# A deep-and-cross network on one core: the row products of the long run split into four products on 32x32 tiles

## The chip, the core and the metric

The kernel runs on one core of one Trainium2 chip. The metric is device time in microseconds (us) for one launch, the median of several runs; lower is better. A profile of one execution lies beside it: a page of tables, and a trace that can be asked for single stretches of time, lines and engines.

## What is computed

Six cross layers over a batch of 16384 rows of 416 features in bfloat16. The reference, cut to what matters:

```python
# x0: (16384, 416), ws: (6, 416, 416), bs: (6, 416), all bf16
x = x0
for l in range(6):
    proj = jnp.einsum('bd,de->be', x, ws[l]) + bs[l]
    x = x0 * proj + x
return x
```

Per layer this is one matrix product with 416 x 416 weights, a bias, a multiplication with x0 and an addition. 416 is 3 x 128 + 32: three full tiles of features and a tail of 32.

## The kernel before, in words

**Layout.** The batch is cut into eight groups of 2048 rows (`GC`), each group into four chunks of 512 rows (`CH`, index j). Activations are kept transposed, features on partitions and batch rows along the free axis, so a product of one layer takes a piece of the weights as the loaded operand and a chunk of 512 rows as the moving operand, and leaves 512 f32 in one PSUM bank. The three full feature tiles lie in `xs` (index t); the tails of the four chunks of a group are stacked as four blocks of 32 partitions in `x3s`. The weights lie in `wm` (three full tiles of input features) and in `w3` (the 32 tail features, four copies, one in each block of 32 partitions).

**Jobs and tiles.** A job is one layer l of one group g. It makes three output tiles of 128 features (i = 0, 1, 2), each in four chunks, and one tail of 32 features. Jobs of different groups are interleaved in a fixed diagonal order. An output chunk needs 416 input features. In the long middle part of the program it is made from row products only: the array is used as four strips of 32 rows and 128 columns, and a product takes 32 input features of one strip r (partitions 32r to 32r+31) against 128 output features. Three full tiles give three such products in each of the four strips, and the tail gives one more in the strip where it lies: 13 products into one bank.

**The searched run.** The function `stream` (line 1005) writes this part. The order of its products is the string `ORDER` (line 204), a result of a search: each letter names a strip and a chunk begun some places ago, and stands for that strip's three or four products of that chunk. `replay` (line 230) turns the string into a list of products by time, with 20 ticks for a product (`SLOT`) and 22 ticks (`FENCE`) between the end of one strip's products of a chunk and the start of the next strip's, as both add into the same bank. In the program the same rule is a semaphore: `Program.add` (line 35) leaves out a dependency between two TensorE instructions on one bank when they have the same `row`, and keeps it as a wait when their rows differ. The run holds 6504 row products: 6000 from line 1040 (full tiles) and 504 from line 1044 (tail features). When a chunk's last product is queued, `evacuate_chunk` (line 538) queues ScalarE's copy from PSUM with the bias (line 550) and, for pairs of chunks, VectorE's multiplication (line 562) and addition (line 567).

**Tail phases.** A "|" in `ORDER` is a tail phase: `tails` (line 677) makes the 32 tail features of two or three jobs. It has 12 products per job on strips of 32 columns and all 128 rows (line 697, form 128*32), and then its corners, four products per job of 32 input by 32 output features (line 685, form 32*32). After the corners the run goes on. There are 14 such phases in the run.

**Elsewhere.** Ahead of the run and behind it the work is done with full products (line 650), row products by `rows32` (line 671, or split in four on 32x32 tiles in its `small` form, line 665) and column products (line 638). The last job is done with batch rows on partitions (line 1130 and after).

**Engines and queues.** TensorE's instructions are in program order; every product is a weight load and a matmul, two instructions. ScalarE and VectorE empty PSUM, SyncE issues nearly all transfers. All waits are semaphores that `Program._solve` places.

The lines that the change touches, with the functions around them:

Of the kernel before, what the change touches and what calls it, by code (L numbers as in the profile page):

```python
# [4 lines left out]
CH = 512  # L5
T32 = 32
# [15 lines left out]
class Program:  # L22
# [12 lines left out]
    def add(self, eng, fn, reads=(), writes=(), lane=None, batch=None, hold=False, release=False, row=None):  # L35
        op = Op(eng, fn, lane, batch, row)
        deps = {}
        if eng == "pool":
            writes = list(writes) + ["pool"]
        for t in reads:  # L40
            w = self.writer.get(t)
            if w is not None:
                deps[id(w)] = (w, True)
        for t in writes:
            w = self.writer.get(t)
            if w is not None:
                deps[id(w)] = (w, True)
            for r in self.readers.get(t, ()):
                if id(r) not in deps:
                    deps[id(r)] = (r, False)  # L50
        for d, raw in deps.values():
            if d.lane is None and d.eng == eng and lane is None and (eng == "pe" or not raw):
                if row is None or d.row is None or row == d.row:
                    continue
            op.deps.append(d)
        for t in reads:
            self.readers.setdefault(t, []).append(op)
        for t in writes:
            self.writer[t] = op
            self.readers[t] = []  # L60
        if eng == "dve":
            if hold:
                self.flush()
                self.held = op
            else:
                self.queue[eng].append(op)
                if release:
                    self.flush()
        else:
            self.queue[eng].append(op)  # L70
        if lane is not None:
            batches = self.lanes.setdefault(lane, [])
            if not batches or batches[-1][0] != batch:
                batches.append((batch, []))
            batches[-1][1].append(op)
        return op
# [229 lines left out]
def bass_standalone__cross_network_dcn__recsys_kernel(  # L306
# [33 lines left out]
    wm = [nc.alloc_sbuf_tensor(f"wm_{l}", [P, NT, D], BF16) for l in range(L)]  # L340
    w3 = [nc.alloc_sbuf_tensor(f"w3_{l}", [P, D], BF16) for l in range(L)]
# [13 lines left out]
    psum = nc.alloc_psum_tensor("ps", [P, 8 * CH], FP32)  # L355

    pr = Program(nc)
    add = pr.add
# [16 lines left out]
    def bank(b, p0=0, p1=P, n=CH):  # L375
        return psum[p0:p1, b * CH:b * CH + n]
# [18 lines left out]
    def wm_tok(l, i):  # L395
        return ("wm", l) if i < 2 else ("wm", l, "rest")
# [41 lines left out]
    def quad(g, l, j):  # L438
        q = (j + turn_of(g, l)) % NJ
        return q, slice(q * T32, (q + 1) * T32)  # L440
# [14 lines left out]
    def x_src(g, l):  # L455

        if l == 0:
            s = slot(g)
            return lambda t, a, b: x0s[s][:, t * GC + a * CH:t * GC + b * CH], lambda t, j: x0_tok(s, t, j)
        s = xset[(g, l)]  # L460
        return lambda t, a, b: xs[s][:, t * GC + a * CH:t * GC + b * CH], lambda t, j: ("x", s, t, j)

    def x3_src(g, l):
        if l == 0:
            s = slot(g)
            return x0s[s][:, XW:XW + CH], x03_toks(s)
        s = xtail[(g, l)]
        return x3s[s][:, :], [("x3", s)]
# [264 lines left out]
    def load_nat(j, k0, k1):  # L733
# [6 lines left out]
        reads=["warm"], writes=["warm"])  # L740
# [229 lines left out]
    def start_job(g, l, ahead=True):  # L970
        started.add((g, l))
        if ahead:
            xset[(g, l + 1)] = free_x.pop(0)
        if (g, l) in W_LOAD:
            load_wm(W_LOAD[(g, l)], "sp")
            load_w3(W_LOAD[(g, l)], "sp")
        if (g, l) in G_LOAD:
            load_group(G_LOAD[(g, l)])
# [26 lines left out]
    def stream(run, keep, part):  # L1005

        chunks = [(it[1], it[2], j) for it in run if it[0] == "tile" for j in range(NJ)]
        due, n = [], 0
        for it in run:
            if it[0] == "tails":  # L1010
                due.append((n, it[1]))
            else:
                n += NJ
        tiles = [it[1:] for it in run if it[0] == "tile"]
        place = {it: NJ * k for k, it in enumerate(tiles)}
        needs = [[(t, place[(g, l - 1), t]) for t in range(NT if c < len(chunks) - keep else part)
                  if c - place.get(((g, l - 1), t), -99) < 30] for c, ((g, l), i, j) in enumerate(chunks)]
        plan, read, left = replay([quad(g, l, j)[0] for (g, l), i, j in chunks], [len(b) for n, b in due],
                                  needs, keep, part)
        at = list(ring)  # L1020
        plan = [(t, r, c, at[b]) if r >= 0 else (t, r, [at[k] for k in c], b) for t, r, c, b in plan]
        left = [at[k] for k in left]
        phases.extend(on for _, r, _, on in plan if r < 0)
        count, seen = {}, {}
        for _, r, c, b in plan:
            if r < 0:
                dve[0] = max(dve[0], phases.pop(0)) + PAIR * len(behind_tail) + TAILS
                tails(due.pop(0)[1], corners_last=True, banks=c)
                continue
            (g, l), i, j = chunks[c]  # L1030
            if (g, l) not in started:
                start_job(g, l, ahead=False)
            count[c] = count.get(c, 0) + 1
            q, ecols = slice(r * T32, (r + 1) * T32), slice(i * P, (i + 1) * P)
            t = seen[c, r] = seen.get((c, r), -1) + 1
            src, stok = x_src(g, l)
            s3, tok3 = x3_src(g, l)
            kw = dict(start=count[c] == 1, stop=count[c] == 4 * NT + 1, tile_position=(r * T32, 0))
            if t < (NT if c < len(chunks) - keep else part):
                add("pe", lambda h, l=l, t=t, j=j, b=b, q=q, ecols=ecols, src=src, kw=kw: h.matmul(  # L1040
                    bank(b), wm[l][q, t, ecols], src(t, j, j + 1)[q, :], **kw),
                    reads=[stok(t, j), wm_tok(l, i)], writes=[("ps", b)], row=r)
            else:
                add("pe", lambda h, l=l, b=b, q=q, ecols=ecols, s3=s3, kw=kw: h.matmul(  # L1044
                    bank(b), w3[l][q, ecols], s3[q, :], **kw),
                    reads=tok3 + [("w3", l, r)], writes=[("ps", b)], row=r)
            if count[c] == 4 * NT + 1:
                evacuate_chunk(g, l, i, j, b, read[c])
        home = {c: b for _, r, c, b in plan if r >= 0}
        ring[:] = sorted(left)  # L1050
        (g, l), i, _ = chunks[-1]
        banks = [home[c] for c in range(len(chunks) - keep, len(chunks))]
        if (g, l + 1) not in xset:
            xset[(g, l + 1)] = free_x.pop(0)
        full(g, l, i, banks, False, True, lambda j: j % 2 and evacuate(g, l, i, banks, [j - 1, j], 2),
             ts_=range(part, NT))
        ring.extend(sorted(banks))
# [20 lines left out]
    for n, it in enumerate(items):  # L1078
        if n == s_lo:
            stream(items[s_lo:s_hi], NJ, 0)  # L1080
# [35 lines left out]
    g, l = LAST, L - 1  # L1116
    src, stok = x_src(g, l)
    s3, tok3 = x3_src(g, l)
# [160 lines left out]
```

## Time and profile before

| what | value |
|---|---|
| median of 3 runs | 467.62 us (467.43 to 467.76) |
| span of the profiled execution, first to last instruction | 465.7 us |
| what lies around the span, against the median | 1.9 us |
| mean granted TensorE clock | 0.997 |
| TensorE matmuls, weight loads | 7827, 7833 |
| TensorE busy | 458.9 us, 99% of the span |
| VectorE busy, ScalarE busy | 404.2 us (87%), 379.1 us (81%) |
| stretch of the run with its tail phases | 40.8 to 429.6 us, 388.8 us |
| line 1040 and line 1044 together | 6504 products |

How to read the profile's lines: a group line gives line of the kernel, engine, operation, output<-inputs, the array form for TensorE (rows*columns), the shape, the count, then busy us and mean ns of one instruction, then the idle time of the engine ahead of them and what ended it. PE is TensorE's matmul, PEld its weight load. Matmuls overlap each other on the array, so busy time is a union and not a sum, and the duration of one matmul is modelled. "Form" below always means rows*columns of the array that a product uses.

### The profile page before, as it was taken

How to read it: one execution, taken by the hardware profiler on the slowest of the kernel's cores; microseconds unless marked ns; L12 is line 12 of the kernel's file. 1: busy time of each engine (PE TensorE's matmuls, PEld its weight loads, DVE VectorE, ACT ScalarE, POOL GpSimd, SP SyncE). 2: the span in 40 equal slices, each digit the busy share in tenths (PEclk: the TensorE clock that was granted, in tenths of full speed). 3: DMA queues.
4: the chain of work that ended last, by engine and by line, in shares of the span. 5: the costliest groups of instructions: out<-in, count | busy, mean ns of one | idle time of the engine just before them, and what ended most of it. 6: DMA issues, size and time to landing. Idle time of an engine off the chain costs nothing.

```text
span 465.7 us, 17469 instructions
## 1 busy us (share of the span) xinstructions
PE 458.9 (99%) x7827; PEld 263.8 (57%) x7833; DVE 404.2 (87%) x700; ACT 379.1 (81%) x608; POOL 6.8 (1%) x15
## 2 busy tenths in 40 slices
PE   9999999999999999999999999999999999999995
PEld 5444566555556677555655556565575566755442
DVE  2887998989989899979989898888989889898897
ACT  4687888788888888888878888788887887889785
POOL 1000000000000000000000000000000000000000
PEclk9999999999999999999999999999999999999998
DMA  8986949101002978084858437990100095027899
GB/s 229 185 177 144 160 113 190 29 3 26 1 4 38 158 210 155 22 141 149 149 92 154 145 78 141 160 296 23 25 2 4 25 148 172 14 49 169 183 161 292
DMA packets 139087, 53.77 MB, mean 115 GB/s; under 512 B 112762, under 2 KB 138500, under 8 KB 139012
## 3 DMA queue, kind: packets, MB, share of 16 engines
q1 hardware_dynamic: 138856, 52.54, 52.5%
q8 instruction: 61, 1.00, 0.9%
q10 hardware_dynamic: 156, 0.11, 0.1%
q14 instruction: 14, 0.11, 0.1%
HBM read 5.97 MB, written 13.63 MB: 42 GB/s over the span
## 4 chain that ended last, share of the span: by engine, by line
PE 93%; DVE 4%; DMA 1%; issue 1%; ACT 0%; SPq 0%; DVEq 0%
PE ps L1040 70%; PE ps L697 7%; PE ps L1044 6%; PE ps L650 6%; PE ps L638 2%; PE ps L685 1%; DMA wm<-in_ws_dram 1%; DVE x L1194 1%; DVE x L1188 1%; DVE x L528 1%; DVE tw L523 1%; PE ps L671 1%; ACT tw L514 0%; PE ps L789 0%; SPq L734 0%
## 5 line engine op out<-in xcount | busy, mean ns | idle before, releaser
L1040 PE MATMUL ps<-x,wm 32*128 32x512 bf16 x6000 | 356.0, 374 | 0.0
L550 ACT ACTIVATE tw<-ps,bias 128x512 bf16<-128x512 f32 x500 | 310.5, 688 | 46.4 <-PE ps L1040 35.9
L1040 PEld LDWEIGHTS ps<-x,wm 32*128 32x128 bf16 x6000 | 212.5, 92 | 127.7 <-ACT tw L550 4.1
L562 DVE TENSOR_TENSOR tw<-tw,x 128x1024 bf16<-128x1024 bf16 x250 | 168.2, 689 | 39.6 <-ACT tw L550 38.9
L567 DVE TENSOR_TENSOR x<-tw,x 128x1024 bf16<-128x1024 bf16 x250 | 163.5, 690 | 0.3
L1044 PE MATMUL ps<-x,w 32*128 32x512 bf16 x504 | 151.7, 374 | 0.0
L1044 PEld LDWEIGHTS ps<-x,w 32*128 32x128 bf16 x504 | 42.7, 92 | 6.6
L514 ACT ACTIVATE tw<-ps,bias 128x512 bf16<-128x512 f32 (+1 forms) x46 | 35.0, 839 | 12.0 <-PE ps L671 7.9
L650 PE MATMUL ps<-x,wm 128*128 128x512 bf16 x146 | 33.6, 379 | 1.0 <-issue 0.8
L697 PE MATMUL ps<-x,wm 128*32 128x512 bf16 x564 | 33.6, 380 | 0.0
L608 ACT ACTIVATE ts<-ps,bias 128x512 bf16<-128x512 f32 x33 | 21.0, 687 | 14.7 <-PE ps L685 14.7
L523 DVE TENSOR_TENSOR tw<-tw,x 128x1024 bf16<-128x1024 bf16 (+1 forms) x35 | 21.4, 627 | 4.9 <-ACT tw L514 4.7
L650 PEld LDWEIGHTS ps<-x,wm 128*128 128x128 bf16 x152 | 13.9, 98 | 19.0 <-issue 3.2
L697 PEld LDWEIGHTS ps<-x,wm 128*32 128x32 bf16 x564 | 13.5, 96 | 18.7 <-ACT tw L550 4.7
L528 DVE TENSOR_TENSOR x<-tw,x 128x1024 bf16<-128x1024 bf16 (+1 forms) x35 | 20.6, 624 | 0.0
L612 DVE TENSOR_TENSOR x<-ts,x 128x512 bf16<-128x512 bf16 x47 | 18.4, 420 | 0.4
L610 DVE TENSOR_TENSOR ts<-ts,x 128x512 bf16<-128x512 bf16 x33 | 13.0, 418 | 0.0
L604 DVE SCALAR_TENSOR_TENSOR ts<-ps,bias,x 128x512 bf16<-128x512 f32 x14 | 10.5, 748 | 2.2 <-PE ps L685 2.2
L909 POOL COPY ost<-ot 128x512 bf16<-128x512 bf16 x6 | 5.3, 890 | 411.3 <-DMA ot<-x 411.3
L1130 PE MATMUL ps<-wm,x 128*128 128x416 bf16 x48 | 9.8, 340 | 0.1
L1182 ACT ACTIVATE x<-ps 128x416 bf16<-128x416 f32 x16 | 7.6, 518 | 2.4 <-PE ps L1130 2.4
L799 DVE COPY x<-ps 128x512 bf16<-128x512 bf16 x5 | 2.0, 423 | 8.5 <-PE ps L789 8.5
(50 smaller groups left out, 76.9 us busy)
## 6 DMA issues: line engine op xcount, KB each, us to landing
out_dram<-ost SPq DMA_DIRECT2D x6, 1664.0 KB, 7.1
x<-x SPq DMA_DIRECT2D x24, 96.0 KB, 2.3
x<-in_x_dram SPq DMA_DIRECT2D x8, 208.0 KB, 4.4
x<-in_x_dram SPq DMA_DIRECT2D x4, 416.0 KB, 8.0
out_dram<-ost SPq DMA_DIRECT2D x2, 832.0 KB, 6.0
wm<-in_ws_dram SPq DMA_DIRECT2D x5, 312.0 KB, 3.4
x<-x SPq DMA_DIRECT2D x22, 64.0 KB, 2.0
out_dram<-x SPq DMA_DIRECT2D x3, 416.0 KB, 4.8
```

The costliest lines, as they stand in the source:

```text
L514: add("act", lambda h, a=a, w=w, b0=b0: h.activation(tw[r][:, a * CH:(a + w) * CH], psum[:, b0 * CH:(b0 + w) * CH], ACT_F.Identity, bias=b ...
L523: add("dve", lambda h, a=a, e=e: h.tensor_tensor(tw[r][:, a * CH:e * CH], tw[r][:, a * CH:e * CH], x0s[s0][:, i * GC + a * CH:i * GC + e * ...
L528: add("dve", lambda h, a=a, e=e: h.tensor_tensor(xs[so][:, i * GC + a * CH:i * GC + e * CH], tw[r][:, a * CH:e * CH], src(i, a, e), ALU.ad ...
L550: add("act", lambda h: h.activation(tw[r][:, j * CH:(j + 1) * CH], bank(b), ACT_F.Identity, bias=bias[:, i, l:l + 1], scale=1.0), reads=[( ...
L562: add("dve", lambda h: h.tensor_tensor(tw[r][:, o], tw[r][:, o], x0s[s0][:, c], ALU.mult), reads=[("tw", r, k) for k in both] + [x0_tok(s0 ...
L567: add("dve", lambda h: h.tensor_tensor(xs[so][:, c], tw[r][:, o], src(i, a, a + 2), ALU.add), reads=[("tw", r, k) for k in both] + [stok(i ...
L608: add("act", lambda h: h.activation(ts[r][:, :], bank(b), ACT_F.Identity, bias=bias[:, 3, l:l + 1], scale=1.0), reads=[("ps", b), "bias"], ...
L612: add("dve", lambda h: h.tensor_tensor(x3s[so][:, :], ts[r][:, :], res, ALU.add), reads=[("ts", r)] + rtok, writes=[("x3", so), ("x3", so, ...
L650: add("pe", lambda h, t=t, j=j, k=k, w=w: h.matmul(bank(banks[j])[:, k * w:(k + 1) * w], wm[l][:, t, ecols], src(t, j, j + 1)[:, k * w:(k ...
L697: add("pe", lambda h, t=t, j=j, src=src, l=l, b=b, ro=ro, qo=qo: h.matmul(psum[qo, b * CH:(b + 1) * CH], wm[l][:, t, NT * P:D], src(t, j, ...
L1040: add("pe", lambda h, l=l, t=t, j=j, b=b, q=q, ecols=ecols, src=src, kw=kw: h.matmul(bank(b), wm[l][q, t, ecols], src(t, j, j + 1)[q, :], ...
L1044: add("pe", lambda h, l=l, b=b, q=q, ecols=ecols, s3=s3, kw=kw: h.matmul(bank(b), w3[l][q, ecols], s3[q, :], **kw), reads=tok3 + [("w3", l ...
```

## The change

Each row product of the run, on 32 rows and 128 columns, becomes four products on 32 rows and 32 columns, one for each strip of 32 columns m. All four read the same moving operand; each loads its own 32 columns of the weights and writes its own 32 partitions of the same PSUM bank. The flags that begin and end the accumulation are those of the row product. Order, banks, waits between strips, evacuation, tail phases, and everything outside the run are as before. `ORDER` and the tick constants are not changed.

```diff
             kw = dict(start=count[c] == 1, stop=count[c] == 4 * NT + 1, tile_position=(r * T32, 0))
             if t < (NT if c < len(chunks) - keep else part):
-                add("pe", lambda h, l=l, t=t, j=j, b=b, q=q, ecols=ecols, src=src, kw=kw: h.matmul(
-                    bank(b), wm[l][q, t, ecols], src(t, j, j + 1)[q, :], **kw),
-                    reads=[stok(t, j), wm_tok(l, i)], writes=[("ps", b)], row=r)
+                lhs, rhs, got = wm[l][q, t, ecols], src(t, j, j + 1)[q, :], [stok(t, j), wm_tok(l, i)]
             else:
-                add("pe", lambda h, l=l, b=b, q=q, ecols=ecols, s3=s3, kw=kw: h.matmul(
-                    bank(b), w3[l][q, ecols], s3[q, :], **kw),
-                    reads=tok3 + [("w3", l, r)], writes=[("ps", b)], row=r)
+                lhs, rhs, got = w3[l][q, ecols], s3[q, :], tok3 + [("w3", l, r)]
+            for m in range(4):
+                o = slice(m * T32, (m + 1) * T32)
+                km = dict(kw, tile_position=(r * T32, m * T32))
+                add("pe", lambda h, b=b, o=o, lhs=lhs, rhs=rhs, km=km: h.matmul(
+                    psum[o, b * CH:(b + 1) * CH], lhs[:, o], rhs, **km),
+                    reads=got, writes=[("ps", b)], row=r)
```

The program has the same 1156 waits of TensorE on its own earlier products as before, and 6504 x 3 = 19512 more matmuls and as many more weight loads, all on TensorE's queue. The other engines' instructions and the transfers of the program are unchanged.

## The prediction

> **What bounds the kernel now.** I read the page's first part, then its costliest groups, then a table by stage.
>
> ```profile
> PE 458.9 (99%) x7827; PEld 263.8 (57%) x7833; DVE 404.2 (87%) x700; ACT 379.1 (81%) x608; POOL 6.8 (1%) x15
> ...
> PE 93%; DVE 4%; DMA 1%; issue 1%; ACT 0%; SPq 0%; DVEq 0%
> ...
> L1040 PE MATMUL ps<-x,wm 32*128 32x512 bf16 x6000 | 356.0, 374 | 0.0
> ```
>
> TensorE is busy 99% of the span, the chain that ended last is 93% TensorE, and line 1040 waits for nothing that counts (0.0 us idle). The table by stage has, per stretch, busy us and count of PE, PEld, DVE, ACT and POOL, then clock, DMA share and GB/s:
>
> ```profile
> 0.00:40.80 40.80, 39.34 (x385) 18.16 (x393) 27.86 (x57) 26.12 (x36) 1.35 (x8) 1.00 0.89 194
> 40.80:429.60 388.80, 388.72 (x7177) 231.90 (x7178) 346.37 (x586) 327.70 (x529) 5.44 (x7) 1.00 0.46 98
> 429.60:465.70 36.10, 30.84 (x270) 13.71 (x270) 29.97 (x59) 25.26 (x46) 0.00 (x0) 0.97 0.91 216
> ```
>
> The change lies wholly in the middle stretch: 388.80 us, of which TensorE is busy 388.72. There VectorE is at 89% and ScalarE at 84%, so neither is the bound. A row product costs 356.0 / 6504 = 54.7 ns (line 1040's union covers line 1044's products too): four strips work at once, so one strip takes 4 x 54.7 = 219 ns for 512 columns.
>
> **What the change adds.** 3 x 6504 = 19512 matmuls and as many weight loads: 39024 instructions. The middle stretch goes from 7177 + 7178 = 14355 instructions of TensorE to 53379, in whatever time it then takes. At the old pace an instruction came every 388.8 us / 14355 = 27.1 ns; to keep that pace one must come every 388.8 us / 53379 = 7.28 ns. So three things have to be asked: can the array do it, can the queue issue it, and can the code be brought in.
>
> *The array.* The nearest row is the `small` form outside the run, line 665, 16 products on the 16 tiles of 32x32, and eight corners right behind them:
>
> ```profile
> 27.09 0.43 PE L665 MATMUL ps<-x,w 32*32 32x512 bf16 x16
> 27.31 0.42 PE L685 MATMUL ps<-x,w 32*32 32x512 bf16 x8
> ```
>
> One product lasts 384 ns there (line 665 by source: 384/384/385) and all 16 together 430, so their starts lie 46 ns apart in all, 3.1 ns each; the next ones on the same tiles begin 0.22 us later, the same as a strip's 219 ns. For the array, sixteen 32x32 products thus cost what four row products cost. I take 0 for the array, with ends of -1.8 us and +14 us (both below). The Trainium skill's page "TensorE: Matmul & The Clock Gate" says, in the section on 56 against 53.3 ns, that matmuls never start closer than about 25 ns however small; the 3.1 ns above speaks against it between different tiles, though in a burst only. By that rule 26016 products would take 650 us in place of 356, an estimate, and the total 762.
>
> *The code.* TensorE's instructions are themselves fetched:
>
> ```profile
> q8 instruction: 61, 1.00, 0.9%
> ```
>
> 61 packets, 1.00 MB. Spread over TensorE's 7827 + 7833 = 15660 instructions that is 64 bytes each, so the queue is TensorE's code (VectorE's 700 and ScalarE's 608 could not fill it), and a packet of 1.00 MB / 61 = 16.4 KB holds 256 instructions. Its 0.9% is of 16 engines' span: 0.009 x 16 x 465.7 / 61 = 1.10 us for one packet. Before, one was needed every 256 x 27.1 ns = 6.9 us, hidden six times over by the array's work. After, the middle stretch needs 53379 / 256 = 208.5 packets, and to stay hidden one must come every 388.8 / 208.5 = **1.86 us**. That cover is thin. If packets follow each other without a gap, 1.10 us each, they are still hidden and cost nothing. If the next is asked for only when a block has been used up, each costs a whole round trip. The trace never shows two on their way at once, since 6.9 us lie between them, so it can't say which. The nearest row for a round trip is the load of similar size from HBM:
>
> ```profile
> w<-in_ws_dram SPq DMA_DIRECT2D x24, 26.0 KB, 2.3
> ```
>
> 2.3 us from issue to landing. So the period of a packet lies between 1.10 us (no gap) and 2.3 + 1.10 = 3.4 us (a round trip and then a transfer), and the middle is also the nearest row, 2.3. I take **2.3 us**: 208.5 x 2.3 = 479.6 us in place of 388.8, which is +90.8. The ends are 0 and 208.5 x 3.4 - 388.8 = +320. The Trainium skill's page "Runtime: NRT & Kernel Launch", section on instruction fetch, says that the fetch is hidden because the sequencer needs some 20 cycles for each instruction; this trace's 1.10 us for 256 is 4.3 ns each, and it shows no issue as slow as that. By that rule (20 cycles at the 1.2 GHz that the page "TensorE: Matmul & The Clock Gate" gives the sequencer, 16.7 ns, an estimate) the stretch would take 890 us and the whole 969.
>
> *Waits.* The 1156 waits of one strip for another stay. What a strip waits for is now the last of four products, issued 3 x 3.1 = 9.3 ns behind the first. ScalarE's evacuation waits for the same last product. Behind a waiting weight load stand the other strips' products in order, so these 9.3 ns hit all strips if nothing is in hand: at most 1156 x 9.3 ns = 11 us, and with the same 9.3 ns on a third as many handovers to ScalarE about 14 us; at least nothing, as a waiting strip has the run's own slack. Where code is late, they are covered by that.
>
> *Forms.* In a tail phase the array goes from row form to 128*32 (line 697), to 32*32 (corners, line 685), and back to rows. Now the last step has one form on both sides.
>
> ```profile
> 57.27 0.42 PE L685 MATMUL ps<-x,w 32*32 32x512 bf16 x12
> 57.62 0.34 PEld L1040 LDWEIGHTS ps<-x,wm 32*128 32x128 bf16 x12 [0.23 <-issue]
> 57.62 0.83 PE L1040 MATMUL ps<-x,wm 32*128 32x512 bf16 x12
> ```
>
> From the corners' start to the next row product it is 0.35 us with a change of form; in the line 665 view the step without one took 0.22. That gives 0.13 us for each of the 14 phases, 1.8 us. It counts only where the array is the bound; if code is, the drain was not what held the run up, and I take 0.
>
> **The sum**, against the profiled execution: 465.7 + 90.8 = 556.5 us of span, and with the 1.9 us by which the median of 467.62 exceeds the span, **558 us**.
>
> **The rivals.**
>
> *The code keeps up* (the other side: faster, or the same). One mechanism: packets come ahead of need, at less than 1.86 us each, and the array's pace stands. For it: 1.10 us for a transfer, and the burst of 3.1 ns per product. Against it: no stretch of the trace shows it sustained. Then only the form is left: 467.6 - 1.8 = 465.8 us. It decides at a packet period of 1.86 us. Chance 0.30: 0.26 faster, 0.04 within 0.2%, which is about what a measurement can tell from no change.
>
> *The code keeps up, but the split delays the handovers between strips.* Price up to 14 us as above less 1.8: 468.6 to 480, likeliest 474. For it: 1156 waits in a stretch without idle time. Against it: a strip's 219 ns are the 0.22 us of the burst, so handovers cost next to nothing now. Chance 0.15.
>
> *Issue is the bound, or code is much later.* The only rate that the trace shows held for long is 27.1 ns an instruction; held, it would give 53379 x 27.1 ns = 1447 us for the stretch, 1526 in all. The other end is the burst, 3.1 ns for a pair. Anything above 760 us needs (760 - 78.8) us / 53379 = 12.8 ns an instruction, 3.3 us a packet. Against it: the rows of line 665 and 685 have 24 pairs on the array within 0.3 us. Chance 0.12.
>
> *The forecast*, code fetch with a period between 1.9 and 3.3 us a packet, that is about 480 to 760 us: chance 0.43. Three of the four cases are slower or far slower, so the sign is more certain than the size.
>
> **Range.** It has to take in the case on the other side, 465.8, so it starts at 463, and reaches to 760, the upper bound of the forecast's own case; left out is the issue-bound case, 0.12. The likeliest case alone would be 480 to 760. Faster by over 0.2%: 0.26; within: 0.04; slower: 0.15 + 0.43 + 0.12 = 0.70.
>
> **What would show it.** Right: about 213 code packets of 16.4 KB (1.00 MB + 39024 x 64 bytes = 3.5 MB), each 256 instructions of TensorE taking clearly over 1.86 us, idle time ahead of the run's weight loads that no engine ended ("issue"), in bursts with a packet's period, and ScalarE and VectorE busy as long as before in a longer span. Wrong: the middle stretch still about 387 us with packets every 1.8 us (the code keeps up); a stretch a few per cent longer with small idle times ended by TensorE's own products (handovers); an even spacing of matmul starts at some fixed number of ns, without bursts (issue). If the corners are followed by the run's products within 0.22 us, the step on forms is right, whatever the total.

## The result, and the profile after

The changed kernel takes 888.59 us (median of 4 runs, 884.76 to 889.32) against 467.52 us before (4 runs): a ratio of 1.899, 95% interval 1.895 to 1.902. It is slower by 421 us, outside the predicted range of 463 to 760 us and far above the 558 us.

First the page of the changed kernel: engine shares, the code queue, the chain that ended last, the run's matmuls (now line 1046), and ScalarE's copies of their results (line 550).

```profile
PE 571.8 (65%) x27339; PEld 397.7 (45%) x27345; DVE 413.5 (47%) x700; ACT 392.6 (44%) x608; POOL 5.9 (1%) x15
...
q8 instruction: 213, 3.49, 1.7%
...
PE 62%; issue 35%; DVE 2%; ACT 0%; DVEq 0%
...
L1046 PE MATMUL ps<-x,wm 32*32 32x512 bf16 x24000 | 470.2, 410 | 285.8 <-issue 284.0
...
L550 ACT ACTIVATE tw<-ps,bias 128x512 bf16<-128x512 f32 x500 | 324.1, 686 | 444.3 <-PE ps L1046 438.1
```

TensorE went from 99% busy to 65%. The new share in the chain is "issue", 35%: time in which TensorE waits for nothing that the profile shows, no semaphore, no other engine, no data. VectorE and ScalarE have as many instructions as before (700 and 608) and are busy little longer (413.5 us against 404.2, 392.6 against 379.1) in a span nearly twice as long, so nothing was added to them; they are starved. ScalarE's copies stood 438.1 us for TensorE's products, against 35.9 us before. The code queue brought 213 packets, as forecast.

The table by stage, of the stretch that the run fills now (columns as before):

```profile
40.80:846.80 806.00, 500.70 (x26680) 365.25 (x26651) 354.66 (x584) 340.22 (x527) 4.50 (x7) 0.92 0.27 52
```

The stretch grew from 388.8 to 806.0 us, which is the whole loss of the profiled run; what lies ahead of it and behind it has not changed. 806.0 / 208.5 packets = 3.87 us a packet.

The chain in order of time, nine microseconds of it (start, length, what):

```profile
231.98 2.04 PE ps L1046 x132
234.02 1.44 issue
235.46 2.03 PE ps L1046 x128
237.49 1.99 issue
239.47 1.53 PE ps L1046 x89
```

These are the lines to look at longest. TensorE works for 2 us, stands for 1.4 to 2 us, and works again, and the piece that lies whole in the window is 128 products: 128 weight loads and 128 matmuls, 256 instructions, as many as a code packet holds. Within a burst the array runs at its full pace: 128 products in 2.03 us, less the 0.41 of the last one, are 12.8 ns each, against 54.7 / 4 = 13.7 for a quarter of a row product. The trace's records of the code queue's packets fit to it: one began at 236.81, 1.35 us after the burst that began at 235.46, took 1.20 us, and the next burst began 1.46 us after it had landed: 1.35 + 1.20 + 1.46 = 4.0 us from burst to burst.

The same holds for the whole run. In the 191 places where TensorE's weight loads pause for more than 0.7 us, the next burst begins a median of 1.38 us after a code packet has landed (1.25 to 1.50 us in the middle four fifths), and the next packet begins a median of 1.14 us after that burst. No two packets overlap: from the landing of one to the start of the next it is at least 2.28 us.

### The profile page after: what moved, and what is told of

The parts are those of the page before. It is cut to its first block, busy times and chain, and to the rows that moved or that the text cites. A ratio compares the mean times of both kernels' runs of the same rounds, so it can differ in the third digit from the quotient of the medians.

```text
span 883.0 us, 56493 instructions
## 1 busy us (share of the span) xinstructions
PE 571.8 (65%) x27339; PEld 397.7 (45%) x27345; DVE 413.5 (47%) x700; ACT 392.6 (44%) x608; POOL 5.9 (1%) x15
## 4 chain that ended last, share of the span: by engine, by line
PE 62%; issue 35%; DVE 2%; ACT 0%; DVEq 0%
PE ps L1046 52%; PE ps L697 4%; PE ps L650 3%; PE ps L638 1%; PE ps L685 1%; DVE x L1196 0%; DVE x L1190 0%; DVE x L528 0%; PE ps L771 0%; DVE tw L523 0%; PE ps L671 0%; PE ps L789 0%; ACT tw L514 0%; ACT tw L550 0%; DVE x L799 0%
## 5 line engine op out<-in xcount | busy, mean ns | idle before, releaser
L1046 PE MATMUL ps<-x,wm 32*32 32x512 bf16 x24000 | 470.2, 410 | 285.8 <-issue 284.0
L1046 PEld LDWEIGHTS ps<-x,wm 32*32 32x32 bf16 x24000 | 345.2, 89 | 396.7 <-issue 357.6
L550 ACT ACTIVATE tw<-ps,bias 128x512 bf16<-128x512 f32 x500 | 324.1, 686 | 444.3 <-PE ps L1046 438.1
L562 DVE TENSOR_TENSOR tw<-tw,x 128x1024 bf16<-128x1024 bf16 x250 | 172.6, 694 | 434.9 <-ACT tw L550 434.7
L1046 PE MATMUL ps<-x,w 32*32 32x512 bf16 x2016 | 185.1, 406 | 19.0 <-issue 18.9
L1046 PEld LDWEIGHTS ps<-x,w 32*32 32x32 bf16 x2016 | 59.3, 89 | 22.0 <-issue 19.3
L697 PE MATMUL ps<-x,wm 128*32 128x512 bf16 x564 | 35.5, 396 | 0.0
L650 PEld LDWEIGHTS ps<-x,wm 128*128 128x128 bf16 x152 | 13.9, 98 | 18.8 <-issue 3.4
L697 PEld LDWEIGHTS ps<-x,wm 128*32 128x32 bf16 x564 | 13.9, 99 | 17.5 <-issue 5.9
L638 PE MATMUL ps<-x,wm 128*32 128x512 bf16 x160 | 9.2, 379 | 0.0
```

Of the source, the lines that this page charges most:

```text
L550: add("act", lambda h: h.activation(tw[r][:, j * CH:(j + 1) * CH], bank(b), ACT_F.Identity, bias=bias[:, i, l:l + 1], scale=1.0), reads=[( ...
L562: add("dve", lambda h: h.tensor_tensor(tw[r][:, o], tw[r][:, o], x0s[s0][:, c], ALU.mult), reads=[("tw", r, k) for k in both] + [x0_tok(s0 ...
L638: add("pe", lambda h, t=t, j=j, c=c, o=o: h.matmul(psum[o, banks[j] * CH:(banks[j] + 1) * CH], wm[l][:, t, i * P + c * T32:i * P + (c + 1) ...
L650: add("pe", lambda h, t=t, j=j, k=k, w=w: h.matmul(bank(banks[j])[:, k * w:(k + 1) * w], wm[l][:, t, ecols], src(t, j, j + 1)[:, k * w:(k ...
L697: add("pe", lambda h, t=t, j=j, src=src, l=l, b=b, ro=ro, qo=qo: h.matmul(psum[qo, b * CH:(b + 1) * CH], wm[l][:, t, NT * P:D], src(t, j, ...
L1046: add("pe", lambda h, b=b, o=o, lhs=lhs, rhs=rhs, km=km: h.matmul(psum[o, b * CH:(b + 1) * CH], lhs[:, o], rhs, **km), reads=got, writes=[ ...
```

## The experiments

Three theories were set against each other. **A (code):** TensorE's instructions arrive in packets of 256, one under way at a time, and the period of a packet (from the start of one to the start of the next) is the bound. **B (issue):** the engine's sequencer needs some 15 ns for each instruction. **C (array and handovers):** products on narrow tiles, with their loads and waits, cost the time on the array.

### Two products of 32x64

```diff
-            for m in range(4):
-                o = slice(m * T32, (m + 1) * T32)
-                km = dict(kw, tile_position=(r * T32, m * T32))
+            for m in range(2):
+                o = slice(m * 2 * T32, (m + 1) * 2 * T32)
+                km = dict(kw, tile_position=(r * T32, m * 2 * T32))
```

> Every row product of the run in two products of 32x64 in place of four of 32x32. The middle stretch has 14355 + 13008 = 27363 instructions of TensorE, 106.9 code packets; the array's 388.8 us give each packet 3.64 us. Theory A (code: one packet of 256 instructions under way at a time, never faster than about 3.4 us, 3.6 to 3.9 on average in the changed kernel): 106.9 x 3.6 to 3.9 = 385 to 417 us, so right at the edge, 468 to 496 us in all, with TensorE idle in bursts where other transfers are heavy. Theory B (issue: each instruction of TensorE takes some 15.1 ns, the changed kernel's 806 us / 53379): 27363 x 15.1 = 413 us, 492 in all, without idle bursts. Theory C (array and handovers: 32-column tiles and the waits between strips cost the time): a third of the changed kernel's 421 us, 140 us more, about 608.

Measured: 517.19 us, ratio 1.107 (1.104 to 1.110). Theory C's 608 is out. Theory A's upper end of 496 was missed too: the stretch took 438.3 us,

```profile
40.80:479.10 438.30, 410.79 (x13682) 266.94 (x13668) 348.98 (x587) 331.78 (x529) 4.66 (x7) 0.99 0.47 89
```

or 438.3 / 106.9 = 4.10 us a packet, more than in the changed kernel. The same transfers of data now fall into half the time (89 GB/s in place of 52), and the packets wait for them; the last experiment comes back to that. Theory B's 492 is not far off, so this run alone does not part A from B.

### Only every fourth chunk split

```diff
-            for m in range(4):
-                o = slice(m * T32, (m + 1) * T32)
-                km = dict(kw, tile_position=(r * T32, m * T32))
+            parts = 4 if c % 4 == 0 else 1
+            for m in range(parts):
+                o = slice(m * P // parts, (m + 1) * P // parts)
+                km = dict(kw, tile_position=(r * T32, m * P // parts))
```

> Only every fourth chunk of the run is split into four products of 32x32, the others keep row products: 14355 + 9756 = 24111 instructions in the stretch, 94.2 packets, for which the array leaves 4.13 us each. Theory A: 94.2 x 3.6 to 3.9 = 339 to 367 us, under 388.8, so the code stays hidden and the kernel takes 467 to 472 us, unless changes of form cost: row form and 32*32 form alternate within the run, at up to 0.1 us each. Theory B: 24111 x 15.1 = 364 us, hidden as well if it is a floor; 421 x 9756 / 39024 = 105 us more, 573 in all, if each instruction adds its share. Theory C: 573 as well.

Measured: 1751.92 us, ratio 3.745 (3.732 to 3.757). All three expectations missed it, and it says nothing of code: its page counts 99 code packets in 1740 us.

```profile
L1047 PE MATMUL ps<-x,wm 32*32 32x512 bf16 (+1 forms) x10500 | 1554.5, 582 | 0.0
L550 ACT ACTIVATE tw<-ps,bias 128x512 bf16<-128x512 f32 x500 | 340.8, 687 | 1253.2 <-PE ps L1047 1250.9
```

The matmul group names two forms and has no idle time, yet ScalarE waits 1250.9 us for it. Chunks at work at the same time are interleaved by strips, so the two forms alternate in the order of the program, 2785 times. The span grew by 1740.5 - 465.7 = 1275 us, 0.46 us for each change, at a granted clock of 0.556. The starts of the matmuls show it directly: from a product of one form to the next of the other it is 0.51 us on average, 1422 us of the 1663 us that the stretch takes here, while two of the same form start a median of 3 ns apart. In the kernel before, it was 0.32 us from the last corner to the first row product, at the full clock. The clause "at up to 0.1 us each" in the expectation was the mistake; the number of instructions can't be dosed by putting a part of the run into another form.

### Half of the columns

```diff
+            n = CH if c >= len(chunks) - keep else CH // 2
             for m in range(4):
...
-                    psum[o, b * CH:(b + 1) * CH], lhs[:, o], rhs, **km),
+                    psum[o, b * CH:b * CH + n], lhs[:, o], rhs[:, 0:n], **km),
```

> The changed kernel with the moving operand cut to 256 of its 512 columns in all chunks of the run but the last four, so half of the run's products is left out; instructions, waits and code are the same. Theory A (code): the time hardly changes, 875 to 890 us, with shorter bursts of work and longer gaps. Theory B (issue): the same 880 to 890, without bursts. Theory C (array, handovers): the array's part of the stretch halves, so some 170 to 200 us less, about 700.

Measured: 896.88 us, ratio 1.917 (1.904 to 1.930). Half of the columns are gone and the time does not fall, it is even 1% above the changed kernel's, and above the 875 to 890 us of theory A. Theory C's 700 us are far off. The table line of the stretch (columns as before) and the run's matmuls:

```profile
40.80:858.00 817.20, 464.01 (x26673) 345.79 (x26672) 353.67 (x585) 337.51 (x527) 3.85 (x7) 0.56 0.27 52
...
L1047 PE MATMUL ps<-x,wm 32*32 32x256 bf16 x24000 | 411.7, 376 | 327.3 <-issue 327.1
```

But the granted clock fell as well, to 0.597 over the run (0.928 in the changed kernel) and 0.56 in the stretch, so that half of the columns at little over half of the clock kept the array busy for nearly as long as before: 464.0 us of the stretch, against 500.7. So this run alone does not rule out the array. It does show the idle time that nothing but "issue" ends, 327.1 us ahead of these matmuls. The next experiment takes the array's time away for good.

### A bare stream, without the network

Five stretches of 2048 products on TensorE with no waits between them, in one execution. The core of it:

```python
for k in range(N): ins = tile(h, k, 512)   # 32x32 tiles, 512 columns
for k in range(N): ins = tile(h, k, 64)    # 32x32 tiles, 64 columns
for k in range(N): ins = row(h, k, 512)    # row products, 512 columns
for k in range(N): ins = row(h, k, 256)    # row products, 256 columns
ins.then_inc(s_pe, 1)                      # SyncE begins to load x0
for k in range(N): ins = tile(h, k, 512)   # as the first
```

> No network: a bare stream on TensorE without waits, five stretches of 2048 products (4096 instructions, 16 code packets each); only x0's first 2048 rows are copied to the output. Stretch 1: 32x32 tiles, 512 columns; 2: 32x32 tiles, 64 columns; 3: row products, 512 columns; 4: row products, 256 columns; 5: like 1, with loads from HBM running beside it. Theory A: stretches 1 and 2 take the same, 16 x 3.4 to 3.6 = 54 to 58 us, in bursts of 128 products; 3 takes the array's 2048 x 54 ns = 110 us; 4, for which the array needs 27 ns a product or 3.46 us a packet, 55 to 60 us; 5 is longer than 1, 16 x 4 to 6 = 64 to 96 us. Theory B (issue, 15.1 ns an instruction): 1, 2, 4 and 5 all 62 us with even spacing, 3 110 us. Theory C (handovers): 1 at the array's 2048 x 13.5 ns = 28 us, 2 shorter, 5 like 1.

The timeline, TensorE's matmuls (start, length, what, idle time before them):

```profile
42.38 3.64 PE L24 MATMUL ps<-x,w 32*32 32x512 bf16 x128 [3.65 <-issue]
48.58 3.65 PE L24 MATMUL ps<-x,w 32*32 32x512 bf16 x128 [2.55 <-issue]
...
69.14 1.99 PE L24 MATMUL ps<-x,w 32*32 32x512 bf16 x128 [2.01 <-issue]
73.14 2.00 PE L24 MATMUL ps<-x,w 32*32 32x512 bf16 x128 [2.01 <-issue]
76.60 2.00 PE L24 MATMUL ps<-x,w 32*32 32x512 bf16 x128 [1.46 <-issue]
...
94.42 1.27 PE L24 MATMUL ps<-x,w 32*32 32x64 bf16 x128 [2.19 <-issue]
98.14 1.27 PE L24 MATMUL ps<-x,w 32*32 32x64 bf16 x128 [2.46 <-issue]
101.60 1.27 PE L24 MATMUL ps<-x,w 32*32 32x64 bf16 x128 [2.18 <-issue]
...
138.43 168.73 PE L30 MATMUL ps<-x,w 32*128 32x512 bf16 x4096
...
367.45 3.64 PE L24 MATMUL ps<-x,w 32*32 32x512 bf16 x128 [0.91 <-issue]
373.39 1.99 PE L24 MATMUL ps<-x,w 32*32 32x512 bf16 x128 [2.29 <-issue]
```

Here, with no waits between products, the bursts are exactly 128 products, nearly every time. From start to start it is 3.46 to 4.0 us in the quiet part, with 512 columns and with 64 alike: an eighth of the columns (at a clock of 0.54 against 0.99, so still only about a quarter of the array's time) makes the burst shorter and the gap longer, and the period stays. So the array's work does not set the period, and neither do waits between strips, as there are none here: theory C is out. Nor is it issue: within a burst of 64-column products the 128 start within 1.27 - 0.22 us, 8.2 ns for a product, 4.1 for an instruction, and theory B's 15.1 ns are out too. While SyncE's stores ran (42 us) the period was 6 to 7 us, while its loads ran (367 us) 4 to 6. The 4096 row products in the middle have no gap at all: with 512 columns a packet lasts the array 111.6 / 16 = 7.0 us, with 256 it still lasts 57.1 / 16 = 3.57, just enough.

```profile
80.33:138.43 58.10, 20.95 (x2081) 18.29 (x2081) 0.00 (x0) 0.00 (x0) 0.54 0.02 5
138.43:250.00 111.57, 111.57 (x2029) 50.66 (x2032) 0.00 (x0) 0.00 (x0) 0.98 0.01 2
250.00:307.10 57.10, 57.10 (x2074) 50.93 (x2066) 0.00 (x0) 0.00 (x0) 1.00 0.02 5
307.10:384.00 76.90, 46.10 (x2051) 31.96 (x2048) 0.00 (x0) 0.00 (x0) 0.72 0.66 203
```

Stretches 2 to 5 took 58.1, 111.6, 57.1 and 76.9 us; theory A had 54 to 58, 110, 55 to 60 and 64 to 96. Stretch 1 took 79 in place of 54 to 58, as the stores of the output ran beside most of it, which the expectation had not counted.

### The same count of instructions without narrow tiles

The kernel before, with the columns of the moving operand halved in place of the tile:

```diff
+            parts = 1 if count[c] == 1 else 2
+            for m in range(parts):
+                o = slice(m * CH // parts, (m + 1) * CH // parts)
+                km = dict(kw, stop=kw["stop"] and m == parts - 1)
+                add("pe", lambda h, b=b, o=o, lhs=lhs, rhs=rhs, km=km: h.matmul(
+                    bank(b)[:, o], lhs, rhs[:, o], **km),
+                    reads=got, writes=[("ps", b)], row=r)
```

> The kernel before with every row product of the run, except the first of each chunk, in two halves of 256 columns of the moving operand: the form stays 32*128, no product moves to another tile, and the array's work is the same. Instructions in the middle stretch: 14355 + 2 x 6000 = 26355, 102.9 code packets. Theory A (code): what counts is the number of instructions alone, so close to the kernel with two products of 32x64 (517.2 us, 438.4 us for 106.9 packets, 4.10 us each): 102.9 x 4.10 = 422 us and 501 in all, 488 to 512. Theory C (32-column or 64-column tiles, their weight loads, handovers): 468 to 472 us, as nothing of that is changed.

Measured: 504.09 us, ratio 1.080 (1.076 to 1.084); 425.3 us for 102.9 packets, 4.13 us each. The form is still 32*128, no tile is narrow, and a packet takes what it took with two products of 32x64 (4.10). More instructions are enough for the loss; narrow tiles are not needed. What the halving itself may cost the array is bounded by the next run.

```profile
L1047 PE MATMUL ps<-x,wm 32*128 32x256 bf16 (+1 forms) x11500 | 370.1, 273 | 18.9 <-issue 17.0
```

### Below the edge

The same in every second chunk only (`parts = 2 if c % 2 == 0 and count[c] > 1 else 1`).

> The same halves of columns in every second chunk only: 14355 + 2 x 3000 = 20355 instructions, 79.5 packets, for which the array leaves 388.8 / 79.5 = 4.89 us each. Theory A: above the 3.5 to 4.3 us that a packet takes in quiet and moderately busy stretches, so hidden but for the few of 6 us: 467 to 474 us. A price for each instruction (the 49.7 us of two products of 32x64 over 13008 instructions, 3.8 ns each): 6000 x 3.8 ns = 23 us more, 490.

Measured: 470.53 us, ratio 1.006 (1.005 to 1.007): 3000 more products, 6000 instructions, for 2.8 us. A price per instruction would have been 23 us. So there is an edge and not a slope: with 4.89 us for a packet the code is hidden, with 3.78 (388.8 / 102.9) it is not.

```profile
L1047 PE MATMUL ps<-x,wm 32*128 32x256 bf16 (+1 forms) x8750 | 359.3, 308 | 0.3 <-issue 0.3
```

### One form after each tail phase, and no more

```diff
                 tails(due.pop(0)[1], corners_last=True, banks=c)
+                fresh[0] = 4
                 continue
...
+            parts = 4 if fresh[0] > 0 else 1
+            fresh[0] -= 1
```

> The kernel before, with only the first four row products after each of the 14 tail phases split into four on 32x32 tiles: 168 products more. The corners and these have one form, and the array changes to row form four products later. Theory A: the code stays hidden (57 packets, 6.8 us each). On forms: the split products start up to 0.3 us earlier than now, but the change of form (0.32 us from one product to the next) now comes behind them, so the time is within 1 us of before, 466.5 to 468.5. If a change of form behind a full round of products were free, 0.3 us x 14 = 4 us less, 463.

Measured: 467.38 us, ratio 0.9995 (0.9986 to 1.0003), no difference. The corners now flow into the run at once, 0.05 us after they begin in place of 0.35, and the change of form comes later. The second group below holds the 16 products on 32x32 tiles and the first 8 row products behind them; the first row product starts at 57.40, 0.31 us after the last of the 16.

```profile
56.83 0.42 PE L685 MATMUL ps<-x,w 32*32 32x512 bf16 x12
56.88 1.13 PE L1049 MATMUL ps<-x,wm 32*32 32x512 bf16 x24
```

### The changed kernel with fewer transfers

```diff
+        if g < LAST - 1:
+            free_x.append(s)
+            free_3.append(s3)
+            return
         turn(0)
```

> The changed kernel without the output of groups 0 to 5 (their turning and their stores are left out; those rows of the output are not written). Instructions of TensorE are the same. Theory A: a code packet takes 3.87 us on average in the changed kernel, 3.68 where no other transfer runs and 4.3 to 6 where many do; with fewer transfers the average falls towards 3.7, so 208.5 x 3.7 = 771 us for the stretch and 850 in all, 840 to 875. Theory B (issue at 15.1 ns an instruction): 888, unchanged.

Measured: 860.33 us, ratio to before 1.839 (1.836 to 1.843), 28 us less than the changed kernel with the same instructions of TensorE. The output of groups 0 to 5 is not written here. The stretch, now with 28 GB/s in place of 52, gives 780.1 / 208.5 = 3.74 us a packet:

```profile
40.80:820.90 780.10, 484.99 (x26663) 360.59 (x26671) 354.02 (x585) 339.39 (x527) 0.10 (x1) 0.95 0.15 28
```

From the records of the changed kernel's code packets: where no other transfer ran, the period had a median of 3.57 us and a mean of 3.68 (some 120 packets); with 100 to 200 GB/s beside it a mean of 4.27 (30); over 200 GB/s 6.0 (8). It is the start of the packet that comes late: sorted by the traffic from a burst to the landing of the next packet, that packet begins 1.18 us after the burst on average without other traffic and 2.94 us beside over 200 GB/s (13 bursts), while its transfer (1.10 and 1.00 us) and the time from its landing to the next burst (1.39 and 1.38 us) stay as they are.

## Why the prediction was wrong

**What bounds the kernel now, and the count.** Right. The forecast was 208.5 packets for the stretch and about 213 in all; 213 came, in bursts with a packet's period, and the whole loss lies there.

**The code.** This is the step that failed. The mechanism was the forecast's, and its deciding sum was mis-sized: "I take **2.3 us**" for a packet. It was 3.87, so the term "+90.8" measured 806.0 - 388.8 = +417. Two things were in it. A period holds a whole round trip: I had that as the upper end, 2.3 + 1.10 = 3.4, and the quiet period is 3.57, of which some 1.1 us pass from the burst to the packet's start, 1.1 in the transfer and 1.4 from its landing to the next burst. I took the middle because a transfer of data of similar size lands in 2.3 us, though nothing in the trace made a code packet one of those. And the packets wait for the data's transfers: 3.87 against 3.68, and 4.10 where the data flow is denser. That other transfers run beside the code was in the profile (DMA share 0.46 in the stretch) and was not in the sum. Even the stated upper end, +320, would have made 788 us; the range was cut at 760, below it, and the 0.12 for "issue is the bound, or code is much later" is where the result fell, by its second half. The trace before held a nearer row than 2.3 us. Its packets lie 6.9 us apart only on average: where one came late, 8.7 to 9.5 us behind the one ahead, the next followed after 3.58, 3.70, 4.15 and 4.78 us, and no two of its 61 packets came closer. With 3.58 the stretch is 208.5 x 3.58 = 746 us and the whole 825.

**The array.** Right: 12.8 ns for a product within a burst. The rule of at least 25 ns between starts on the Trainium skill's page "TensorE: Matmul & The Clock Gate" is not what this case shows between different tiles: 8.2 ns in the bare stream, for 128 products in a row.

**Issue.** The rival's rate was no floor. On the Trainium skill's page "Runtime: NRT & Kernel Launch" the section on instruction fetch mechanics says that the fetch is hidden behind a slower issue. In these runs it is the other way round: issue went at 4.1 ns an instruction, and the fetch, at 3.57 us for 256 instructions or 13.9 ns each, stood in front of it. Its 969 us was nearer than my 558 all the same, as 16.7 ns an instruction happens to lie near the 15.1 that the fetch gave.

**Waits.** The up to 14 us for handovers can't be seen: where code is late there is slack. The kernel with halves in every second chunk has the same 1156 waits and hidden code, and all its costs together are 2.8 us, but its two halves run on the same strip, not on four tiles. No run shows the term itself; it stays open.

**Forms.** Right in sign. In the changed kernel the first product of the run starts 3 to 14 ns after the last corner in all 14 phases, against 317 before; I had given it 0.13 us a phase. The timeline of one phase:

```profile
73.37 0.82 PE L697 MATMUL ps<-x,wm 128*32 128x512 bf16 x12
74.12 0.42 PE L685 MATMUL ps<-x,w 32*32 32x512 bf16 x12
74.17 0.80 PE L1046 MATMUL ps<-x,wm 32*32 32x512 bf16 x23
```

Up to 0.31 x 14 = 4.3 us were to be had, a hundredth of what the code cost. And the kernel with the split only after each phase shows that there the change of form is merely put off. None of the kernels here beats the kernel before.

**What stays open.** The trace shows that a packet begins some 1.1 us after the burst before it has begun and that the next burst starts some 1.4 us after it has landed; what happens in these two times it doesn't show. In none of the traces do two packets overlap, and at least 2.2 us lie between the landing of one and the start of the next. Whether two could be under way together was not tried; no run shows it.

## What to carry to other kernels

Count TensorE's instructions before splitting products: divide them by the packet's 256, and compare the time that the array takes for a packet with its period here, some 3.6 us in quiet and 4 to 6 beside heavy transfers. Where the array needed longer than the period, splitting was nearly free (2.8 us for 6000 instructions); where it needed less, every packet cost the full period, whatever the products did. Where a resource has never been the bound in a trace, look for the places where it had to catch up, take the upper end of its cost and not a middle, and add what the other users of the same engines will take. And don't alternate two forms within a run to get a part of a gain: each change of form took 0.3 to 0.5 us.

## What the runs showed of the hardware that was not expected

- TensorE's code comes in packets of 16.4 KB, 256 instructions; one takes 1.1 us to move and, where TensorE stands for it, 3.46 to 4.0 us from one burst to the next in the quiet part of the bare stream, up to 7 us beside stores. A stream that uses them up faster stands with "issue" as its only sign. Other traffic delays a packet's start (1.18 us after the burst in quiet, 2.94 beside over 200 GB/s), not its transfer.
- The granted clock was lower in most runs in which TensorE worked in bursts: 0.928 in the changed kernel, 0.597 with half of the columns, 0.54 in the bare stream's 64-column stretch, though 0.99 in its quiet bursts of 512 columns (57 to 80 us). The period of a packet hardly moved with it, 817.2 / 208.5 = 3.92 us with half of the columns against 3.87, since the array was not the bound.
- With a change of form every few products TensorE's granted clock was 0.556 and each change took about half a microsecond, while the page showed it 100% busy: busy time did not tell of it, ScalarE's wait of 1250.9 us did.
